# A softmax-attention and Mish kernel: order of all engines planned anew, six blocks of exps moved from ScalarE to VectorE, the second group's queries made later, the dense branch in other groups

## Chip, cores, metric

The kernel runs on one core of one Trainium2 chip. The metric is the device time of one execution in microseconds (us), lower is better. Each ratio compares runs on one chip. PE is TensorE's matmuls, PEld its weight loads, ACT is ScalarE, DVE VectorE, POOL GpSimd, SP SyncE. L891 is line 891 of the kernel; the lines of the changed kernel are numbered five higher (L896), and those of some experiments a few higher again.

## The reference

Attention with 32 heads of 20 dimensions over 2048 tokens, and beside it a dense branch with a Mish activation; a sigmoid gate per token mixes the two.

```python
def _A_ref(x, wqkv, wo):                     # x: 1 x 2048 x 640
    q, k, v = (x @ wqkv) ...                 # 32 heads of 20
    p = softmax(q k^T * 20 ** -0.5)
    return (p v) ... @ wo
def _B_ref(x, w1, b1, w2):                   # 640 -> 1536 -> 640
    h = x @ w1 + b1
    return (h * tanh(log1p(exp(h)))) @ w2    # cut: written there in its stable form
g = sigmoid((x * gate_w).sum(-1))
return g * a + (1 - g) * b                   # both on A_x
```

## The kernel before

The work is cut into 33 groups: four heads by 512 queries (the last group is halved into groups 31 and 32). A group has 16 blocks of 128 keys. For each block TensorE makes scores into a two-bank PSUM buffer (two heads of 512 queries), and either ScalarE takes exps of it, or VectorE makes an approximate exp out of integer steps; TensorE then multiplies the result with the values. `SHARE` says how many blocks of each group VectorE takes.

```python
SHARE = (3, 6, 5, 2, 5, 4, 4, 6, 3, ...)     # one number for each group
def dve_keys(G):
    n = SHARE[G]
    if G >= NG - 2:                          # the two half groups take blocks in pairs
        return [DVE_KEYS[i:i + 2] for i in range(0, n - 1, 2)]
    return [(j,) for j in (DVE_KEYS[2:2 + n] if G == 0 else DVE_KEYS[:n])]

# ScalarE: one exp for two heads of a block (1024 columns, PSUM to SBUF)
nc.scalar.activation(eb.tile[:, 0:w * QC], sb.tile[:, 0:w * QC], ACT.Exp, scale=inv)
...
te.__init__("ACT", 55 + 0.833 * w * QC, ex, [ts, prev], prio=2, key=n, rings=[eb], frees=[sb])

# VectorE: for two heads of a block, and then two shifted copies of all four
nc.vector.tensor_scalar(out=bufs[0].tile[...], in0=xb.tile, scalar1=..., scalar2=..., ...)
...
(nc.vector ...).tensor_scalar(out=bufs[i].tile[...], in0=bufs[0].tile[...], scalar1=float(SHIFTS[i]), ...)
```

All engines' instruction order is fixed while the program is built. A planner (`class Order`) holds a list of tasks with costs in ns, keeps a clock for each engine and picks the next task by priority and thresholds; the tasks are issued in the order it finds. `DENSE`, `KEYS`, `OUT` and the like say from which group on a task may be picked (`at(3.5)`: when half the exps of group 3 are issued). Where TensorE would be idle, the planner puts filler matmuls with a zero weight to keep its clock up. Three two-bank buffers (`S`) hold scores for both engines.

```python
LOW, AHEAD, HOLD, BESIDE, AHEAD_D = 2, 24, 650, 30, 2000      # one a line in the kernel
...
end = S[1].before.end or self.now["ACT"] + 908 * (S[1].key - self.exp - 1)
...
for G in list(range(1, NQ)) + [g_of(NP - 1, c) for c in range(NQ)]:
    q_unit(G, at(G - 0.85 if G > 1 else 0.15), prio=2.5, key=G)
```

The softmax here doesn't subtract the row's maximum and nothing guards it: scores larger than these inputs give would overflow.

## Time and profile before

| | before |
|---|---|
| time, median of 4 runs | 799.9 us (798.3 to 804.8) |
| span of the profiled run | 797.9 us |
| busy PE / DVE / ACT | 763.0 / 686.7 / 760.6 us |
| first exp starts; last exp ends | 11.3; 779.7 us |

The prediction below shows the busy shares, the costly groups and the waits. One more view is wanted, the busy time by stretches of the span (columns: stretch and its length, then busy us and instructions of PE, PEld, DVE, ACT and POOL, the clock, the DMA share, GB/s):

```profile
0.00:20.00 20.00, 15.98 (x198) 8.35 (x198) 6.99 (x21) 11.29 (x13) 9.24 (x10) 1.00 0.93 313
20.00:40.00 20.00, 19.15 (x418) 9.70 (x416) 16.86 (x28) 14.47 (x16) 0.00 (x0) 1.00 0.60 199
40.00:60.00 20.00, 19.63 (x290) 6.91 (x286) 17.00 (x29) 19.22 (x22) 0.00 (x0) 1.00 0.09 23
```

ScalarE is the fourth pair: 14.47 of 20 us from 20 to 40, while TensorE has 19.15. In the opening ScalarE waits for TensorE.

### The profile page before, as it was taken

Reading aid. Unit: us, or ns where it says so; the run is one execution under the profiler, and the core shown is the slowest. Engines: PE = TensorE matmul, PEld = TensorE weight load, DVE = VectorE, ACT = ScalarE, POOL = GpSimd, SP = SyncE. Lnnn points to the kernel's source line nnn. Section 1 sums busy time; section 2 is a strip of 40 time slices with the busy share of each in tenths; the row PEclk is TensorE's granted clock in tenths of the full one; section 3 lists DMA queues with packets and bytes.
Section 4 is the critical chain, followed back from the end, with each engine's and each line's share of the span. In section 5 each row is a group of like instructions: output and inputs, shape, how many; then the busy total and the mean of one; then the engine's idle time right before and its main releaser. Section 6 shows DMA issues by size and latency. Waiting matters only on the chain.

```text
span 797.9 us, 25753 instructions
## 1 busy us (share of the span) xinstructions
PE 763.0 (96%) x11326; PEld 272.7 (34%) x11326; DVE 686.7 (86%) x910; ACT 760.6 (95%) x789; POOL 9.8 (1%) x12
## 2 busy tenths in 40 slices
PE   7999999999899999899999999989999998999987
PEld 4432223323433223432333323243322233333355
DVE  3889988897799978898999998988898888989964
ACT  5799999999999999999999999999999999999991
POOL 4000000000000000000000000000000000000000
PEclk9999999999999999999999999999999999999999
DMA  9600220111011100011210121100010002202123
GB/s 312 201 23 21 46 58 21 27 36 52 28 40 38 36 19 22 6 47 38 62 42 21 31 64 44 31 23 28 23 36 17 20 19 85 69 19 82 37 67 108
DMA packets 47096, 39.88 MB, mean 50 GB/s; under 512 B 20580, under 2 KB 41252, under 8 KB 46984
## 3 DMA queue, kind: packets, MB, share of 16 engines
q1 hardware_dynamic: 46040, 37.80, 16.6%
q8 instruction: 88, 1.44, 0.7%
q10 hardware_dynamic: 944, 0.45, 0.2%
q14 instruction: 24, 0.20, 0.1%
HBM read 26.63 MB, written 11.08 MB: 47 GB/s over the span
## 4 chain that ended last, share of the span: by engine, by line
PE 49%; ACT 38%; DVE 7%; DMA 3%; issue 3%; SPq 1%; POOL 0%; DVEq 0%; ACTq 0%
ACT es L891 28%; PE S L866 18%; PE C L849 13%; PE X L585 10%; ACT arena L1072 8%; DVE t L925 3%; PE X L668 2%; PE S L585 2%; DVE t L939 1%; DMA rows<-rec 1%; DMA rbc<-rows 1%; PE X L625 1%; PE X L647 1%; ACT L1072 1%; ACT L1071 1%
## 5 line engine op out<-in xcount | busy, mean ns | idle before, releaser
L891 ACT ACTIVATE es<-S 128x1024 bf16<-128x1024 f32 x738 | 680.3, 1128 | 13.8 <-PE S L866 13.4
L925 DVE TENSOR_SCALAR t<-S 128x1024 uint16<-128x1024 f32 x286 | 348.1, 1219 | 38.9 <-PE S L866 37.4
L866 PE MATMUL S<-qs,kt 32*128 32x512 bf16 (+1 forms) x2112 | 302.6, 376 | 15.2 <-ACT es L891 11.3
L939 DVE TENSOR_SCALAR t<-t 128x2048 uint16<-128x2048 uint16 x286 | 189.3, 684 | 7.2 <-PE C L849 5.5
L866 PEld LDWEIGHTS <-kt 32*128 32x128 bf16 x2112 | 90.6, 91 | 288.3 <-issue 280.3
L849 PE MATMUL C<-es,va 128*32 128x512 bf16 (+1 forms) x1524 | 134.8, 380 | 1.0 <-DVE oraw L973 0.6
L849 PE MATMUL C<-t,vs 128*32 128x512 bf16 (+1 forms) x1176 | 102.0, 379 | 2.2 <-DVE t L939 1.6
L585 PE MATMUL X<-w,arena 128*32 128x320 bf16 x1536 | 78.3, 302 | 0.2
L585 PE MATMUL X<-xt,w 128*32 128x512 bf16 x960 | 74.8, 383 | 2.6 <-DVE arena L1058 1.4
L849 PEld LDWEIGHTS <-va 128*32 128x32 bf16 x2112 | 47.2, 95 | 66.7 <-issue 61.7
L1072 ACT ACTIVATE arena<-arena 128x2048 bf16<-128x2048 bf16 x36 | 69.2, 1944 | 0.3
L849 PE MATMUL C<-t,va 128*32 128x512 bf16 (+1 forms) x588 | 56.9, 379 | 0.0
L585 PEld LDWEIGHTS <-arena 128*32 128x32 bf16 x1856 | 40.2, 95 | 40.2 <-issue 31.6
L668 PE MATMUL X<-xt,wqk 128*32 128x512 bf16 (+1 forms) x640 | 49.5, 383 | 1.5 <-DVE g L674 1.2
L1058 DVE TENSOR_SCALAR arena<-X,b 128x512 bf16<-128x512 f32 x48 | 35.8, 745 | 6.2 <-PE X L585 6.2
L849 PEld LDWEIGHTS <-vs 128*32 128x32 bf16 x1176 | 28.5, 95 | 31.4 <-issue 27.9
L585 PEld LDWEIGHTS <-w 128*32 128x32 bf16 (+1 forms) x1280 | 27.2, 95 | 33.4 <-issue 27.8
L585 PE MATMUL X<-wvt,xt 128*32 128x160 bf16 x1240 | 27.8, 233 | 4.7 <-DVE va L725 3.9
L1026 DVE TENSOR_TENSOR on<-oraw,rbc 128x512 bf16<-128x512 f32 (+1 forms) x32 | 21.7, 679 | 11.8 <-DMA rbc<-rows 11.6
L585 PEld LDWEIGHTS <-xt 128*32 128x32 bf16 x1280 | 23.3, 96 | 15.3 <-issue 13.5
L463 PE MATMUL C<-wqk,gw 128*32 128x512 bf16 (+4 forms) x380 | 26.3, 368 | 0.0
L674 DVE CAST g<-X 120x512 bf16<-120x512 f32 x32 | 21.8, 681 | 2.1 <-PE X L668 2.1
(80 smaller groups left out, 250.6 us busy)
## 6 DMA issues: line engine op xcount, KB each, us to landing
rbc<-rows SPq DMA_DIRECT2D x124, 64.0 KB
w<-in_B_w_dram SPq DMA_DIRECT2D x2, 1920.0 KB
out_dram<-xt SPq DMA_DIRECT2D x16, 160.0 KB
oc<-on SPq DMA_DIRECT2D x112, 20.0 KB
arena<-in_A_x_dram SPq DMA_DIRECT2D x3, 640.0 KB
k<-g SPq DMA_DIRECT2D x16, 120.0 KB
kt<-k SPq DMA_DIRECT2D x24, 80.0 KB
q<-g SPq DMA_DIRECT2D x16, 120.0 KB
```

What stands on the lines that cost most here:

```text
L463: nc.tensor.matmul(t[32 * r:32 * r + 32, a:a + n], lhsT=gw[:, 0, 1:33], rhs=wqk[:, r, 0:n], start=G is None, stop=G is None, tile_position ...
L585: nc.tensor.matmul(t[32 * r:32 * r + 32, 0:width], lhsT=lhsT(r), rhs=rhs, start=a, stop=b, tile_position=(0, 32 * r))
L668: nc.tensor.matmul(t[32 * r:32 * r + w, 0:QC], lhsT=wqk[:, k, a:a + w], rhs=xt[:, c, k, :], start=k == 0, stop=k == KT - 1, tile_position= ...
L674: nc.vector.tensor_copy(out=gb.tile, in_=t[0:120, 0:QC])
L849: nc.tensor.matmul(acc[G][32 * r:32 * r + 32, qa:qb], lhsT=vs4[:, b, term - 1, DVE_KEYS.index(j), h:h + 32] if term else va4[:, b, j, h:h ...
L866: nc.tensor.matmul(t[:, (off + a) * QC + i * w:(off + a) * QC + (i + 1) * w], lhsT=kt[32 * r:32 * r + 32, (p % 2) * S + j * P:(p % 2) * S ...
L891: nc.scalar.activation(eb.tile[:, 0:w * QC], sb.tile[:, 0:w * QC], ACT.Exp, scale=inv)
L925: nc.vector.tensor_scalar(out=bufs[0].tile[:, 2 * QC * hp:2 * QC * (hp + 1)], in0=xb.tile, scalar1=P * LOG2E * inv, scalar2=P * (127 - log ...
L939: (nc.vector if eng == "DVE" else nc.gpsimd).tensor_scalar(out=bufs[i].tile[:, a * w:(a + 1) * w], in0=bufs[0].tile[:, a * w:(a + 1) * w], ...
L1026: nc.vector.tensor_tensor(out=nb.tile[:, qa:qb], in0=ob.tile[:, qa:qb], in1=rb.tile[:, qa:qb], op=ALU.mult)
L1058: lambda t: nc.vector.tensor_scalar(out=hs[:, ft, :], in0=t[:, 0:QC], scalar1=b1[:, ft:ft + 1], scalar2=None, op0=ALU.add),
L1072: nc.scalar.activation(v, hs[:, 4 * a:4 * a + 4, :] if i == 0 else v, func, bias=1.0 if i == 1 else 0.0)
```

## The change

It intends a shorter program by the same forms of instructions in another order: the planner is told a longer time for an exp (below, the new pitch), six blocks move from ScalarE to VectorE, and group 1's queries are made later. The core of the diff (left out: two `908` to `915` more, the clause for `IDLE`, which is never true, and literals that became entries of `STEPS` with the same value):

```diff
-SHARE = (3, 6, 5, 2, 5, 4, 4, 6, 3, 5, 5, 5, 5, 5, 4, 4, 6, 4, 3, 6, 5, 4, 5, 4, 5, 4, 6, 4, 5, 4, 3, 4, 4)
+SHARE = (3, 4, 5, 4, 5, 5, 5, 4, 5, 5, 5, 6, 3, 4, 4, 5, 5, 6, 4, 6, 5, 4, 4, 6, 5, 6, 6, 5, 4, 4, 3, 3, 6)
-DENSE = (1.25, 4.7, 11.7, 18.4)
+DENSE = (1.75, 4.25, 9.3, 14.95)
-MISH = (2.4, 4.2, 0.25, 3.7)
+MISH = (2.2, 4.1, 0.5, 2.55)
-DOWN = (-0.85, -1.2, 4.15, 7.5)
+DOWN = (-0.85, -0.55, 3.3, 7.0)
-KEYS = ((0, 0.8, 1.45), (1, 5.2, 7.45), (2, 13.05, 14.0), (3, 17.65, 18.85), (4, 24.55, 25.05))
+KEYS = ((0, 0.35, 1.75), (1, 5.2, 7.75), (2, 12.45, 12.8), (3, 17.8, 18.1), (4, 23.35, 23.55))
-VALUES = ((1, 3.1), (2, 10.6), (3, 12.7))
+VALUES = ((1, 4.6), (2, 10.6), (3, 12.1))
-OUT = (26.05, 27.7, 27.55)
+OUT = (29.85, 30.05, 26.65)
-    LOW = 2
+    LOW = 3
-    AHEAD = 24
+    AHEAD = 6
-    HOLD = 650
+    HOLD = 350
-    BESIDE = 30
-    AHEAD_D = 2000
+    BESIDE = 120
+    IDLE = 1000000000.0
+    AHEAD_D = 1600
-            end = S[1].before.end or self.now["ACT"] + 908 * (S[1].key - self.exp - 1)
+            end = S[1].before.end or self.now["ACT"] + 915 * (S[1].key - self.exp - 1)
-        q_unit(G, at(G - 0.85 if G > 1 else 0.15), prio=2.5, key=G)
+        q_unit(G, at(G - STEPS[4] if G > 1 else 0.45), prio=2.5, key=G)
-        te.__init__("ACT", 55 + 0.833 * w * QC, ex, [ts, prev], prio=2, key=n, rings=[eb], frees=[sb])
+        te.__init__("ACT", 62 + 0.833 * w * QC, ex, [ts, prev], prio=2, key=n, rings=[eb], frees=[sb])
```

More of the change, by code (lines that the diff above doesn't have):

```diff
@@ L34 @@
 DVE_KEYS = (1, 4, 7, 10, 13, 14)
-SHARE = (3, 6, 5, 2, 5, 4, 4, 6, 3, 5, 5, 5, 5, 5, 4, 4, 6, 4, 3, 6, 5, 4, 5, 4, 5, 4, 6, 4, 5, 4, 3, 4, 4)
-DENSE = (1.25, 4.7, 11.7, 18.4)
-MISH = (2.4, 4.2, 0.25, 3.7)
-DOWN = (-0.85, -1.2, 4.15, 7.5)
-KEYS = ((0, 0.8, 1.45), (1, 5.2, 7.45), (2, 13.05, 14.0), (3, 17.65, 18.85), (4, 24.55, 25.05))
+SHARE = (3, 4, 5, 4, 5, 5, 5, 4, 5, 5, 5, 6, 3, 4, 4, 5, 5, 6, 4, 6, 5, 4, 4, 6, 5, 6, 6, 5, 4, 4, 3, 3, 6)
[3 more added lines that the diff above has]
+KEYS = ((0, 0.35, 1.75), (1, 5.2, 7.75), (2, 12.45, 12.8), (3, 17.8, 18.1), (4, 23.35, 23.55))
 QUERIES = 2.05
-VALUES = ((1, 3.1), (2, 10.6), (3, 12.7))
-OUT = (26.05, 27.7, 27.55)
+VALUES = ((1, 4.6), (2, 10.6), (3, 12.1))
+OUT = (29.85, 30.05, 26.65)
+STEPS = (2.8, 2.0, 0.2, 0.6, 0.85, 1.7)
 PAIRS = 8
@@ L195, in pick_pe @@
         if S and S[1].before2:
-            end = S[1].before2.end or self.now["ACT"] + 908 * (S[1].key - self.exp - 2)
+            end = S[1].before2.end or self.now["ACT"] + 915 * (S[1].key - self.exp - 2)
             if not (S[1].before2.end and S[1].before2.end <= now) and len(self.spare.free) < S[1].key - self.exp:
@@ L206, in pick_pe @@
                     end = free[1][0]
-                last = 0 if self.mode == "row" else (S[1].before.end or self.now["ACT"] + 908 * (S[1].key - self.exp - 1)) - self.EARLY
+                last = 0 if self.mode == "row" else (S[1].before.end or self.now["ACT"] + 915 * (S[1].key - self.exp - 1)) - self.EARLY
                 S = max(S[0], min(end + self.LAT["ACT"], last)), S[1]
@@ L223, in pick_pe @@
         if S and S[1].before:
-            end = S[1].before.end or self.now["ACT"] + 908 * (S[1].key - self.exp - 1)
+            end = S[1].before.end or self.now["ACT"] + 915 * (S[1].key - self.exp - 1)
             over = max(lim, end - self.EARLY)
-        if X and X[1].due + self.LATE < self.visit:
+        if X and (X[1].due + self.LATE < self.visit or
+                  X[1].due <= self.visit and self.now["DVE"] + self.IDLE < now):
             lim = min(lim, X[0])
@@ L709, in q_fetch @@
         t_q[G] = o.add("SP", 4000, fetch, t_zero + [t_qd[u, c] for u in {u for _, u, _ in pieces(p)}],
-                       after=at(G - 1.7), prio=1, key=G - 0.5, rings=[q_buf[G]])
+                       after=at(G - STEPS[5]), prio=1, key=G - 0.5, rings=[q_buf[G]])
         t_q[G].issue = 1150
@@ L825 @@
         for i, js in enumerate(((0, 1, 2), (3, 4, 5), (6, 7, 8), (9, 10, 11), (12, 13, 14), (15,))):
-            v_unit(b, js, at(a + 0.2 * i), a + 0.2 * i)
+            v_unit(b, js, at(a + STEPS[2] * i), a + STEPS[2] * i)
     t_sel = o.add("POOL", 2000, make_sel, [t_k[7, j] for j in range(NS)] + list(t_kd.values()), prio=2)
@@ L1192 @@
         for ft in range(FT):
-            h_unit(c, ft, at(base + 2.8 * ft / FT), base)
+            h_unit(c, ft, at(base + STEPS[0] * ft / FT), base)
         mish(c, base + MISH[c])
@@ L1196 @@
             for hf in range(2):
-                b_unit(c, u, hf, at(base + DOWN[c] + 2.0 * (2 * u + hf) / 8), base + 4)
+                b_unit(c, u, hf, at(base + DOWN[c] + STEPS[1] * (2 * u + hf) / 8), base + 4)
     free_of = {c: [] for c in range(NQ)}
@@ L1211 @@
             for hf in range(2):
-                f_unit(c, u, hf, at(OUT[c] + 0.6 * (2 * u + hf) / 8), 29 + c)
+                f_unit(c, u, hf, at(OUT[c] + STEPS[3] * (2 * u + hf) / 8), 29 + c)
     ORDER.append(o.run())
```

## The prediction

> **What bounds the kernel now.** I read the page's busy shares first, then the slices, then the groups by line, then the waits of each engine, and last the timeline of the opening and of the end.
>
> ```profile
> PE 763.0 (96%) x11326; PEld 272.7 (34%) x11326; DVE 686.7 (86%) x910; ACT 760.6 (95%) x789; POOL 9.8 (1%) x12
> ...
> PE   7999999999899999899999999989999998999987
> PEld 4432223323433223432333323243322233333355
> DVE  3889988897799978898999998988898888989964
> ACT  5799999999999999999999999999999999999991
> ```
>
> ScalarE (ACT) has a 5 in the first slice, a 7 in the second, a 1 in the last, and nines between. Its idle time is 797.9 - 760.6 = 37.3 us. By stretches of the trace it lies so: 8.7 us in the first 20 us, 5.5 us from 20 to 40, 16.2 us after 780, 0.8 us from 760 to 780, and about 6 us in all the 720 us between. So in the body ScalarE is 99% busy: **the body lasts as long as ScalarE's work in it**.
>
> TensorE's 96% says less. 26.3 us of it (L463, 380 matmuls) are fillers that multiply a zero weight to keep the clock up, and a busy time that joins the modelled ends of short matmuls counts their latency too. VectorE has 14% free.
>
> ```profile
> L891 ACT ACTIVATE es<-S 128x1024 bf16<-128x1024 f32 x738 | 680.3, 1128 | 13.8 <-PE S L866 13.4
> L925 DVE TENSOR_SCALAR t<-S 128x1024 uint16<-128x1024 f32 x286 | 348.1, 1219 | 38.9 <-PE S L866 37.4
> ...
> L939 DVE TENSOR_SCALAR t<-t 128x2048 uint16<-128x2048 uint16 x286 | 189.3, 684 | 7.2 <-PE C L849 5.5
> ...
> L849 PE MATMUL C<-t,vs 128*32 128x512 bf16 (+1 forms) x1176 | 102.0, 379 | 2.2 <-DVE t L939 1.6
> ...
> L1072 ACT ACTIVATE arena<-arena 128x2048 bf16<-128x2048 bf16 x36 | 69.2, 1944 | 0.3
> ```
>
> The reader is to see two things. An exp lasts 1128 ns but is worth 680.3/738 = 0.922 us of the engine, since neighbours overlap. And ScalarE waited 13.4 us in all for scores (L866), while VectorE waited 37.4 us for them: the plan already serves ScalarE first.
>
> ```profile
> PEld L866 <- issue: 280.3, 732, 1.8
> ...
> ACT es L891 <- PE S L866: 13.4, 15, 2.9
> ...
> PE S L866 <- ACT es L891: 11.3, 23, 1.5
> ```
>
> Of these waits, the largest (2.9 us) is in the opening, and with the next four it makes 8.1 us between 12 and 60 us. Before it the timeline has:
>
> ```profile
> 17.57 0.61 PE L647 MATMUL X<-xt,wvt 128*32 128x512 bf16 x8
> ...
> 18.50 0.61 PE L647 MATMUL X<-xt,wvt 128*32 128x512 bf16 x8
> ...
> 24.65 1.26 PE L625 MATMUL X<-xt,wvt 128*32 128x512 bf16 x20
> ...
> 27.20 2.15 ACT L891 ACTIVATE es<-S 128x1024 bf16<-128x1024 f32 x2 [2.94 <-PE S L866]
> ```
>
> L647 here makes the second group's queries, and they sit in front of the third chunk's keys (L625 at 24.65) for which ScalarE then waits.
>
> **What the Trainium skill says.** "ScalarE: Activation LUTs", section "What ACT_TABLE_LOAD costs", gives 186 ns + 0.833 ns per element for an activation with immediate scale and bias, and says neighbours overlap by some 93 ns. For 1024 elements that is an estimated pitch of 186 + 853 - 93 = 946 ns; the trace has 922, so the slope agrees and the fixed part is a little smaller with this source. The same section gives 1283 ns for a table load; the trace's eight loads at L1071 and L1072 take 1283 each. "VectorE: DVE Perf Modes", section "The perf-mode tier table", gives 693 ns for a 2048-element bf16 tensor_scalar in SBUF and a lower mode for PSUM sources; the trace's 684 (L939) and 1219 for only half the elements out of PSUM (L925) agree. "Perfetto Trace Analysis", section "Identifying the Most-Contended Engine", says that occupancy is a fair measure for ScalarE and VectorE and that matmul busy share is not one for TensorE; the 26.3 us of fillers in this trace show why.
>
> **The change part by part.** No instruction's form changes. What changes is who takes which block of scores, and the order.
>
> (1) *The shares.* SHARE says how many of a group's 16 key blocks VectorE exponentiates. In the first 31 groups the sum goes from 139 to 145. The last two groups take blocks in pairs and round down: before 2 and 2 pairs, after 1 and 3, the same four. So six blocks move. A block is two exps on ScalarE (two of four heads each): 31 x 16 = 496 blocks, (496 - 139) x 2 + 24 = 738 exps before, which is the count in the row, and (496 - 145) x 2 + 24 = 726 after. **ScalarE loses 12 exps: 12 x 0.922 = 11.1 us.** Since it is 99% busy in the body, that is on the path.
>
> VectorE gains two L925 and two L939 a block: 6 x 2 x (1.217 + 0.662) = 22.5 us, with the busy time of each group divided by its count. It goes from 686.7 to about 709 us. Between 20 and 780 us it has 760 us and is busy about 671 now; 693 then, 91%. That lies beside ScalarE's work as long as it keeps up. TensorE's score tiles are as many as before (12 fewer for ScalarE, 12 more for VectorE); each moved block adds eight scaled-value matmuls (1176 = 8 x 147 blocks now), 48 x 102.0/1176 = 4.2 us of TensorE. It can displace fillers, of which there are 26.3 us.
>
> (2) *Order constants.* 908 to 915 ns, and 55 to 62, put the planned exp nearer to the traced 922. They change no work, only what order is found: 738 x 7 ns = 5.2 us by which the old plan let ScalarE run early. The old order already leaves only 6 us of ScalarE idle in the body, so a truer order has at most those 6 us to win there. The other thresholds (HOLD, BESIDE, AHEAD, LOW) have no sign that the profile shows; the new IDLE is so large that its clause can never be true.
>
> (3) *The opening.* The second group's queries are opened at 0.45 of the first group, not 0.15. The three pieces of L647 in front of the stall last 0.40 + 0.61 + 0.61 = 1.6 us, so the wait of 2.94 us can fall by about that. The rest of those 8.1 us has other causes, and the same matmuls have to run before group 1 needs them. I count **-2 us, between -4 and 0**.
>
> (4) *The dense branch.* Its four chunks open at 1.75, 4.25, 9.3 and 14.95, not 1.25, 4.7, 11.7 and 18.4: the same 36 activations of 1.94 us and eight table loads, in other groups. The sum on ScalarE does not change, and I expect the number of loads to stay eight, since only the first piece of Ln and of Tanh switches. What it can change is TensorE's fit: now fillers take 6.4 us in the stretch 640 to 680 and 5.1 us in 520 to 560, where the activations are thick, so the work is uneven.
>
> (5) *The end.* OUT goes from 26.05 and 27.7 to 29.85 and 30.05 for the first two chunks of the output. That looks like a delay, but now the first of their mixes (L1145 on X) runs only at 741.7 us, in the last groups anyway. From the last exp (about 779.7) to the end are 18 us of projection matmuls, mixes and stores, which the change does not touch: 0, within 1 us.
>
> The sum: -11.1 - 2, and **+2 to +3 for new waits of ScalarE**, because VectorE at 91% holds its score buffers at more awkward moments (three two-bank buffers serve both engines). Net about -10.6 us of the profiled span. On the timed median that is 801.2 - 10.6 = 790.6. Because a better-fitted order may also take a part of the 6 us of body idle, I put it at **790.0 us**, a gain of 1.4%.
>
> **The rivals.**
> *A: the work that leaves ScalarE returns as waits.* VectorE or the three shared score buffers become the bound in dense groups; ScalarE's waits for L866 rise from 13.4 to over 20 us. For it: VectorE already waited 37.4 us for scores, so TensorE cannot always serve both. Against it: the fillers show spare TensorE time. It would make 795 to 801 us.
> *B: everything falls into place.* The opening yields its 4 us and the body its idle, on top of the exps: 801.2 - 11.1 - 4 - 2 = about 784. For it: the opening's stall has one plain cause. Against it: body idle is already under 1%, and more VectorE work makes it harder to keep.
> *C: TensorE is the true bound, and ScalarE merely keeps pace.* Then 12 fewer exps are worth nothing and 4.2 us more matmuls cost: 801 to 806. For it: TensorE's slices are all nines, and from 700 to 740 both are 100% busy. Against it: 26.3 us of fillers, and ScalarE seldom waits for it.
>
> **Range and chances.** B's end lies near 783, A's near 799; I take 782 to 798 for 8 in 10. Over 2% faster means under 785.2, which takes 16 us: the exps, the whole opening and some body idle. I give that 0.19, within 2% 0.78, slower by over 2% (above 817) 0.03.
>
> **What would show each step right or wrong.** L891 x726 with busy near 669 us, and a total of ScalarE near 749.5, show (1); L925 and L939 x298 and VectorE near 709 show its other side. ScalarE's waits for L866 under 16 us keep rival A out; over 20 us are rival A. The first 40 us should hold 12 us of ScalarE idle, not 14.2, for (3). Table loads at L1071 and L1072 should be eight; each more costs 1.28 us. From the last exp to the end should be 17 to 19 us for (5). The prediction is wrong if the span stays within 3 us of the old one though the exps are 12 fewer, or if it falls by over 16 us, which no term of my sum holds.

## The result, and the profile after

The changed kernel runs at **788.4 us** (median of 4, 787.7 to 790.6) against 799.9 before (798.3 to 804.8). The ratio is 0.985, 95% interval 0.980 to 0.990. A ratio here is the mean time of one kernel's runs over that of the other's of the same rounds, so not quite the ratio of the medians. The output is right.

Of the page after, the busy shares and the groups that answer to those shown before:

```profile
PE 754.6 (96%) x11346; PEld 267.3 (34%) x11346; DVE 706.0 (90%) x934; ACT 751.3 (96%) x777; POOL 9.7 (1%) x12
...
L896 ACT ACTIVATE es<-S 128x1024 bf16<-128x1024 f32 x726 | 671.0, 1069 | 12.8 <-PE S L871 12.1
L930 DVE TENSOR_SCALAR t<-S 128x1024 uint16<-128x1024 f32 x298 | 363.2, 1220 | 21.3 <-PE S L871 19.7
...
L944 DVE TENSOR_SCALAR t<-t 128x2048 uint16<-128x2048 uint16 x298 | 197.6, 684 | 6.4 <-PE C L854 4.2
...
L854 PE MATMUL C<-t,vs 128*32 128x512 bf16 (+1 forms) x1224 | 110.4, 378 | 3.2 <-DVE t L944 3.0
...
L1077 ACT ACTIVATE arena<-arena 128x2048 bf16<-128x2048 bf16 x36 | 68.7, 1928 | 0.3
```

Twelve exps fewer (726), twelve instructions more in each of VectorE's two rows, 48 matmuls more. VectorE waits 19.7 us for scores, not 37.4. ScalarE waits 12.1 us, hardly less than 13.4.

The busy time by stretches after, the same three:

```profile
0.00:20.00 20.00, 15.82 (x254) 8.46 (x254) 8.30 (x25) 11.35 (x13) 9.24 (x10) 1.00 0.91 308
20.00:40.00 20.00, 18.75 (x354) 8.69 (x352) 14.48 (x22) 17.59 (x20) 0.00 (x0) 1.00 0.63 205
40.00:60.00 20.00, 19.99 (x298) 6.39 (x295) 19.40 (x33) 19.92 (x22) 0.00 (x0) 1.00 0.08 22
```

ScalarE has 17.59 us in the second stretch, 3.1 more. The timeline after shows the stall there shrunk:

```profile
23.32 1.26 PE L630 MATMUL X<-xt,wvt 128*32 128x512 bf16 x20
...
25.88 4.69 ACT L896 ACTIVATE es<-S 128x1024 bf16<-128x1024 f32 x5 [1.63 <-PE S L871]
```

The keys of the first heads are made in four chunks of 512. The third chunk's (then L625 at 24.65) start at 23.32 and ScalarE waits 1.63 us, not 2.94. Group 1's queries (L652) now run at 32.3 us, no longer from 15.4 to 18.9; whether that is why, experiment 4 asks.

**A ledger.** Busy and idle time cannot say where 11.3 us of span went, because a wait shorter than the tail of the exp before it is not idle: exps overlap. So I took the start of each exp from the trace, and its distance to the next start. Where nothing holds ScalarE back, that distance is the same all through: 904 ns, in 485 of the distances before and 437 after to within 5 ns (170 in each lie between 911 and 929, most of them at about 920; what sets these is not known). What is above 904 ns I call the **excess**; it is the waits, those hidden under a tail too, and those 16 ns. (Of the 13 distances that hold Mish activations or the gate's exp, what exceeds their usual length counts; that is about 2 us in each kernel, and the rows do not hang on it.)

| us | before | after | difference |
|---|---|---|---|
| start of the first exp | 11.3 | 10.6 | -0.6 |
| exps x 0.904 | 667.2 | 656.3 | **-10.9** |
| excess, 0 to 20 us | 0.1 | 0.8 | +0.7 |
| excess, 20 to 60 us | 7.5 | 3.4 | **-4.1** |
| excess, 60 to 760 us | 15.3 | 20.4 | **+5.1** |
| excess after 760 us | 1.3 | 0.1 | -1.2 |
| end of the last exp to the end | 18.3 | 18.0 | -0.3 |
| Mish activations, table loads, the rest | 76.9 | 77.0 | +0.1 |
| span | 797.9 | 786.6 | -11.3 |

In this account the 12 exps are the gain; the opening gives four more, and the body takes them back as waits. Whether the exps are also the cause, the experiments ask. (The profiled run of the kernel before had 3.41 us at half clock from 282.8 us on, beside which lie some 1.3 us of its excess; that of the changed kernel had none before its end. So without it the body's rise would be nearer to 6 us.)

### The profile page after: what moved, and what is told of

Same layout as the page of the kernel before. It is cut to its first block, busy times and chain, and to the rows that moved or that the text cites.

```text
span 786.6 us, 25802 instructions
## 1 busy us (share of the span) xinstructions
PE 754.6 (96%) x11346; PEld 267.3 (34%) x11346; DVE 706.0 (90%) x934; ACT 751.3 (96%) x777; POOL 9.7 (1%) x12
## 4 chain that ended last, share of the span: by engine, by line
PE 49%; ACT 31%; DVE 12%; DMA 3%; issue 3%; SPq 1%; POOL 0%; DVEq 0%; ACTq 0%
ACT es L896 22%; PE S L871 18%; PE C L854 14%; PE X L590 11%; ACT arena L1077 8%; DVE t L930 5%; DVE t L944 3%; PE X L673 2%; DMA rbc<-rows 2%; PE S L590 1%; DMA rows<-rec 1%; DMA wvt<-in_A_wqkv_dram 1%; ACT L1077 1%; ACT L1076 1%; DVE on L1031 1%
## 5 line engine op out<-in xcount | busy, mean ns | idle before, releaser
L896 ACT ACTIVATE es<-S 128x1024 bf16<-128x1024 f32 x726 | 671.0, 1069 | 12.8 <-PE S L871 12.1
L930 DVE TENSOR_SCALAR t<-S 128x1024 uint16<-128x1024 f32 x298 | 363.2, 1220 | 21.3 <-PE S L871 19.7
L944 DVE TENSOR_SCALAR t<-t 128x2048 uint16<-128x2048 uint16 x298 | 197.6, 684 | 6.4 <-PE C L854 4.2
L871 PEld LDWEIGHTS <-kt 32*128 32x128 bf16 x2112 | 83.6, 91 | 277.0 <-issue 266.7
L854 PE MATMUL C<-es,va 128*32 128x512 bf16 (+1 forms) x1500 | 131.0, 378 | 1.5 <-DVE oraw L978 0.8
L854 PE MATMUL C<-t,vs 128*32 128x512 bf16 (+1 forms) x1224 | 110.4, 378 | 3.2 <-DVE t L944 3.0
L854 PEld LDWEIGHTS <-va 128*32 128x32 bf16 x2112 | 49.4, 95 | 69.5 <-issue 60.7
L854 PE MATMUL C<-t,va 128*32 128x512 bf16 (+1 forms) x612 | 59.5, 377 | 0.4 <-DVE t L930 0.4
L854 PEld LDWEIGHTS <-vs 128*32 128x32 bf16 x1224 | 31.7, 95 | 36.2 <-issue 31.0
L590 PEld LDWEIGHTS <-xt 128*32 128x32 bf16 x1280 | 23.3, 96 | 15.4 <-issue 13.8
L468 PE MATMUL C<-wqk,gw 128*32 128x512 bf16 (+4 forms) x352 | 25.4, 352 | 0.0
L978 DVE COPY oraw<-C 128x512 f32<-128x512 f32 (+1 forms) x33 | 22.0, 667 | 0.7 <-PE C L854 0.6
```

The source lines that it names most:

```text
L468: nc.tensor.matmul(t[32 * r:32 * r + 32, a:a + n], lhsT=gw[:, 0, 1:33], rhs=wqk[:, r, 0:n], start=G is None, stop=G is None, tile_position ...
L590: nc.tensor.matmul(t[32 * r:32 * r + 32, 0:width], lhsT=lhsT(r), rhs=rhs, start=a, stop=b, tile_position=(0, 32 * r))
L854: nc.tensor.matmul(acc[G][32 * r:32 * r + 32, qa:qb], lhsT=vs4[:, b, term - 1, DVE_KEYS.index(j), h:h + 32] if term else va4[:, b, j, h:h ...
L871: nc.tensor.matmul(t[:, (off + a) * QC + i * w:(off + a) * QC + (i + 1) * w], lhsT=kt[32 * r:32 * r + 32, (p % 2) * S + j * P:(p % 2) * S ...
L930: nc.vector.tensor_scalar(out=bufs[0].tile[:, 2 * QC * hp:2 * QC * (hp + 1)], in0=xb.tile, scalar1=P * LOG2E * inv, scalar2=P * (127 - log ...
L944: (nc.vector if eng == "DVE" else nc.gpsimd).tensor_scalar(out=bufs[i].tile[:, a * w:(a + 1) * w], in0=bufs[0].tile[:, a * w:(a + 1) * w], ...
```

## The experiments

Theory: ScalarE bounds the body, so 12 exps fewer are 11 us. Rivals: TensorE is the true bound; the gain is the new order's and not the exps'; the new planned pitch alone is enough. Twelve kernels ran, on four chips, each with its own runs of the kernel before (medians 800.1, 799.5, 798.4 and 798.7). The last table of this section has them all.

### 1. As much less for ScalarE in both kernels, order untouched

Each exp runs on 1006 of 1024 columns. The planner's cost is not changed, so all engines' orders stay. (The columns that are left out are set once at the start.)

```diff
-            nc.scalar.activation(eb.tile[:, 0:w * QC], sb.tile[:, 0:w * QC], ACT.Exp, scale=inv)
+            nc.scalar.activation(eb.tile[:, 0:w * QC - 18], sb.tile[:, 0:w * QC - 18], ACT.Exp, scale=inv)
```

> The kernel before with its order untouched, each of its 738 exps shortened by 18 of 1024 columns (15 ns at 0.833 ns a column, so 738 x 15 = 11.1 us less for ScalarE, the same as the 12 exps that the change takes away). Results are wrong on purpose. Theory (ScalarE is the bound of the body): the time falls by 9 to 11 us, ratio to the kernel before 0.986 to 0.989, though nothing was planned anew. Rival C (TensorE is the true bound): it stays within 3 us, ratio above 0.996. Rival 'the new order, not the smaller share, brings the gain': ratio above 0.993.

> The changed kernel, order untouched, its 726 exps shortened by the same 18 columns: 726 x 15 = 10.9 us less for ScalarE. If ScalarE is still the bound after the change, the time falls by 8 to 11 us, to 777 to 780 us, ratio to the kernel before 0.971 to 0.976, and ScalarE's waits for scores grow by under 3 us. If VectorE or TensorE has become a bound beside it, under half of it comes (above 783 us), and ScalarE's waits grow by over 5 us.

Measured: the kernel before goes to 794.8 us, ratio 0.994 (0.991 to 0.998); the changed one to 785.3, ratio 0.9815 (0.979 to 0.984). The rows of exps, first of the one before, then of the changed one:

```profile
L894 ACT ACTIVATE es<-S 128x1006 bf16<-128x1006 f32 x738 | 672.8, 1068 | 16.7 <-PE S L869 15.5
```

```profile
L899 ACT ACTIVATE es<-S 128x1006 bf16<-128x1006 f32 x726 | 665.6, 1029 | 13.9 <-PE S L874 12.8
```

The distance of exps that nothing holds back is now 888 ns, so the cut itself arrived: 16 ns each, 11.8 and 11.6 us. But the excess rose, from 24.2 to 31.4 us and from 24.7 to 32.2. The idle column shows only a part of that (15.5 us against 13.4, and 12.8 against 12.1). **This speaks against my theory as I had put it**: the same cut gives 5.4 of 11.8 us in the old order, 3 to 4 of 11.6 in the new (3.1 by the medians, 4.0 by the spans). By the marks set beforehand, 0.994 is the reading "the new order, not the smaller share" (over 0.993), though with an interval that reaches into the gap between it and the theory; and 785.3 is the reading that another engine bounds beside ScalarE, though the waits of over 5 us that were to show it appear in the excess (7.5 us) and not in the idle column (0.7). ScalarE is a bound of the body, but not the only one.

### 2. Which engine takes it back

Here the changed kernel is made lighter on the other engines, order untouched. For TensorE the value matmuls (all but a group's first and last) run on 480 of 512 columns; for VectorE its two steps run on 500 of 512 columns a head in 30 of the 33 groups, and the value matmuls are 12 columns shorter with them.

```diff
+                cut = 32 if 0 < k < total - 1 and G < NG - 2 else 0
-                    nc.tensor.matmul(acc[G][32 * r:32 * r + 32, qa:qb],
+                    nc.tensor.matmul(acc[G][32 * r:32 * r + 32, qa:qb - cut],
```

```diff
+                m = QC if G in (13, NG - 2, NG - 1) else QC - 12
                 nc.vector.tensor_scalar(
-                    out=bufs[0].tile[:, 2 * QC * hp:2 * QC * (hp + 1)], in0=xb.tile,
+                    out=bufs[0].tile[...].rearrange("p (h q) -> p h q", q=QC)[:, :, 0:m],
+                    in0=xb.tile.rearrange("p (h q) -> p h q", q=QC)[:, :, 0:m],
```

> The changed kernel, order untouched; 724 of the weighted-value steps (all but a group's first and last) run on 480 of 512 columns, so TensorE has 724 x 32/2.4 ns = 9.7 us less to do and ScalarE and VectorE the same. Wrong results on purpose. If TensorE bounds the body beside ScalarE, the time falls by 2 to 6 us below 788.4 (ratio 0.977 to 0.983) and ScalarE's excess over back-to-back exps, 24.7 us in the changed kernel, falls. If ScalarE alone is the bound, it stays within 1.5 us and the excess stays at 23 to 26 us.

> The lighter TensorE and the exps of 1006 columns together, order untouched; wrong on purpose. The shorter exps alone gave 3 us of 10.9 in the changed kernel. If it was TensorE's load that took the rest back, the same cut is now worth 6 us or more over the run with the lighter TensorE alone, and the time is under 779 us (ratio under 0.973). If it was the fixed order itself (a score that comes late because of what stands before it, not because TensorE is full) or VectorE, the cut is worth 2 to 4 us again, and the time is 780 to 784.

> The changed kernel, order untouched, with the exps of 1006 columns (10.9 us less for ScalarE) and VectorE's two steps on 500 of 512 columns a head in 30 of the 33 groups (25 + 13 ns for 282 pairs of instructions, 10.6 us less; the matmuls that read them are 12 columns shorter, 3.8 us less for TensorE). Wrong on purpose. The shorter exps alone gave 785.3 us, with a lighter TensorE 782.8. If VectorE took the rest back, the time is 776 to 780 us (ratio 0.970 to 0.976). If it did not, it is 782 to 785 (above 0.977).

> All three at once, order untouched: ScalarE 10.9 us less, VectorE 10.6 us less, TensorE about 10 us less. Wrong on purpose. If the three engines bound different stretches of one tight order, only this gives the whole cut: 776 to 779 us, ratio 0.970 to 0.974. If something that none of the three cuts touches takes it back (the times from one engine to the next, transfers, the dense branch's matmuls), it stays at 780 to 783.

Measured: 786.1, 782.8, 781.2 and 778.8 us (ratios 0.982, 0.978, 0.978, 0.976; the first two and the last two on one chip each). The cuts arrived: a step of four value matmuls starts 202 to 203 ns after the one before it where it was 216 (32 columns at 0.42 ns), and VectorE's two steps take 1195 and 672 ns on average, not 1220 and 684. The row of exps with all three lighter:

```profile
L900 ACT ACTIVATE es<-S 128x1006 bf16<-128x1006 f32 x726 | 660.5, 1048 | 12.5 <-PE S L875 12.1
```

A lighter TensorE alone gives 2 us, by the ratios (0.985 to 0.982), of the 9.7 taken off, and the excess falls to 22.9 us: just inside the reading "TensorE bounds beside ScalarE". With the shorter exps as well, the excess is 31.6 us, and with shorter exps and a lighter VectorE 30.3: hardly under the 32.2 of the shorter exps alone. (Both traces have a stretch of 3.4 us at half clock in the opening, with 1.5 us more of excess in the first 20 us than the changed kernel; the second has one more at 110 us.) So neither TensorE nor VectorE alone holds back the cut, and the two expectations are no clean "yes": 782.8 was within "the fixed order or VectorE", 781.2 between the two ranges. With all three lighter the excess is 25.6 us, about that of the changed kernel, and the span is 10.1 us shorter for cuts of 10 to 11.6. By the ratios (0.985 to 0.976) it is only about 7 us, with 4 us of uncertainty on the first ratio alone; 778.8 lies in the range set for "only all three give the whole cut", 0.976 above it (0.970 to 0.974). So most of the cut comes, and whether all of it does is not shown; a part may be taken back by what no cut touched, such as the times from one engine to the next. On one chip, the shorter exps give 3.3 us beside the lighter TensorE (786.1 to 782.8), and the lighter TensorE gives 2.3 us beside the other two (781.2 to 778.8): each of these adds about a quarter of itself. **The three engines share the bound**: that each is the last at some places of this order is the reading that fits, and ScalarE's time alone counts at about a third.

### 3. The fillers

The fillers on the accumulator are left out; order untouched.

```diff
-            for r in range(4):
+            for r in range(4 if G is None else 0):
                 nc.tensor.matmul(t[32 * r:32 * r + 32, a:a + n], lhsT=gw[:, 0, 1:33], rhs=wqk[:, r, 0:n],
```

> The changed kernel, order untouched, without the filler matmuls on the accumulator (about 25 us of TensorE's busy time). If they only lie in TensorE's spare time (so the change's 48 added matmuls have room) the time stays within 2 us of the changed kernel's 788, ratio 0.983 to 0.988, and TensorE's busy time falls by over 15 us. If TensorE is the bound, the time falls by over 5 us. If the clock is granted less without them, the clock in the records falls below 0.98 and the time rises.

Measured: 798.4 us, ratio 0.998 (0.994 to 1.001): 10 us slower than the changed kernel. The clock by slices and the mean clock, the page's line and the list of cores:

```profile
PEclk9999989999999999989999999989999999899999
```

```profile
core 0: 798.4 us, clock 0.983
```

The trace has four stretches of 6.83 us at half clock in the body, where the changed kernel's profiled run has none before its end. Excess: 35.9 us. As the order is the same, each exp can be set against the same exp of the changed kernel: from the first exp to the last it falls back by 11.2 us, of which 8.6 at these four stretches. So the third reading is right in kind, though the clock (0.983 in the profiled run, 0.983 to 0.991 in all four) stayed just above the 0.98 that was set: left out and replaced by nothing, the fillers cost clock. Whether real work may take their place is another question, which this does not test; the changed kernel has 48 value matmuls more and 28 fillers fewer (352, not 380) at a clock of 0.999.

### 4. The opening

The changed kernel with one number set back; all is planned anew.

```diff
-        q_unit(G, at(G - STEPS[4] if G > 1 else 0.45), prio=2.5, key=G)
+        q_unit(G, at(G - STEPS[4] if G > 1 else 0.15), prio=2.5, key=G)
```

> The changed kernel with the second group's queries opened at 0.15 again, not 0.45; the whole order is planned anew from that, so later parts differ too. Step 3 of the prediction: ScalarE's idle time in the first 40 us rises by 1 to 4 us (it is 11.1 us in the changed kernel, 14.2 in the one before), and the time with it, to 789 to 793 us. Rival (the opening's gain comes from the other order constants): the first 40 us stay at 11 to 12 us of idle. The time beyond the first 60 us may move by a few us either way, as a plan that was tuned as a whole is disturbed.

Measured: 794.1 us, ratio 0.992 (0.989 to 0.995), a little above the range set. ScalarE's idle time in the first 40 us is 13.9 us, 2.8 more than in the changed kernel, as expected. Its stretch from 20 to 40 us:

```profile
20.00:40.00 20.00, 19.21 (x398) 9.14 (x390) 16.55 (x26) 15.26 (x18) 0.00 (x0) 1.00 0.60 196
```

ScalarE is busy 15.26 us there, 17.59 in the changed kernel; the excess in the stretch is 5.2 against 2.8 us. Later kernels agree: with the late queries 2.8 us (experiment 5's old shares, and the searched one), with the early ones 6.1 and 6.2 (the other two of experiment 5), 6.2 in the kernel before; but those differ in other numbers too. So the later queries are worth **2.4 us** there, the plan around them included.

Not by the wait that the prediction named, though. With the queries early again (L652), the exp after the third chunk's keys still waits only 1.65 us, and the loss lies at the fourth chunk's:

```profile
19.04 1.05 PE L652 MATMUL X<-xt,wvt 128*32 128x512 bf16 x16
...
23.85 1.25 PE L630 MATMUL X<-xt,wvt 128*32 128x512 bf16 x20
...
26.40 5.61 ACT L896 ACTIVATE es<-S 128x1024 bf16<-128x1024 f32 x6 [1.65 <-PE S L871]
...
32.14 1.43 PE L630 MATMUL S<-xt,wvt 128*32 128x512 bf16 x20
...
35.09 5.69 ACT L896 ACTIVATE es<-S 128x1024 bf16<-128x1024 f32 x6 [3.09 <-PE S L871]
```

In the changed kernel the fourth chunk's keys start at 29.17, in two pieces, and the exp after them waits less:

```profile
29.17 0.61 PE L630 MATMUL S<-xt,wvt 128*32 128x512 bf16 x8
...
30.09 0.83 PE L630 MATMUL S<-xt,wvt 128*32 128x512 bf16 x12
...
32.27 8.36 ACT L896 ACTIVATE es<-S 128x1024 bf16<-128x1024 f32 x9 [0.79 <-PE S L871]
```

So the fall from 2.94 to 1.65 us at the third chunk comes without the late queries, from other numbers of the change, and the late queries save 2.3 us at the fourth (3.09 to 0.79; 2.10 in the kernel before). The profiled span is 4.3 us longer than the changed kernel's: 2.3 us of excess from 20 to 60 us, 0.5 us of a later first exp, and some 1.5 us beyond 60 us, where the plan is disturbed. (By the ratios the kernel is some 5.7 us slower; the profiled run was the fastest of its four.)

### 5. The shares, the pitch, and fewer exps in an order not tuned to them

Each is planned anew from other numbers: the changed kernel with `SHARE` of before; the kernel before with the new pitch alone; the kernel before with the new `SHARE`, `DENSE`, `MISH`, `DOWN`, `KEYS`, `VALUES` and `OUT` but the old pitch, thresholds and opening.

```diff
-SHARE = (3, 4, 5, 4, 5, 5, 5, 4, 5, ...)    # the changed kernel
+SHARE = (3, 6, 5, 2, 5, 4, 4, 6, 3, ...)    # with the shares of before
```

```diff
-        te.__init__("ACT", 55 + 0.833 * w * QC, ...    # the kernel before; 908 likewise
+        te.__init__("ACT", 62 + 0.833 * w * QC, ...    # with the new pitch alone; 915 likewise
```

> The changed kernel with SHARE as before: 738 exps, planned anew with the new constants and places. Theory (the 12 exps are the gain): 10.9 us more of ScalarE, 797 to 803 us, ratio 0.995 to 1.003. Rival (order and places bring the gain): 787 to 792, ratio under 0.990. Since a plan tuned as a whole is disturbed, ScalarE's excess may rise too; it is counted apart from the exps.

> The kernel before with the new pitch alone (915 for 908 ns, 62 for 55) and planned anew. If the truer pitch by itself brings the gain: 786 to 792 us, ratio under 0.990. Theory: it takes no work from ScalarE, the count stays 738, and the time is 796 to 806, ratio 0.995 to 1.007.

> The kernel before with the new SHARE and the new places of the dense branch, keys, values and output, but the old pitch, order constants and opening; planned anew. It has 726 exps. If fewer exps are enough, whatever the order, it runs at 787 to 792 us like the changed kernel (ratio under 0.990). If the gain needs an order that keeps ScalarE fed, ScalarE's excess over back-to-back exps rises well above 25 us and the time is 794 to 806 us.

None isolates its number cleanly, as a plan that was tuned as a whole is disturbed each time. Measured: old shares 811.8 us (ratio 1.015, 1.010 to 1.020); the pitch alone 807.4 (1.011, 1.005 to 1.017); new shares and places 800.6 (1.003, 1.001 to 1.004, 20 runs). The first two are slower than any range set for them (797 to 803, and 796 to 806). The row of exps of the last:

```profile
L891 ACT ACTIVATE es<-S 128x1024 bf16<-128x1024 f32 x726 | 672.3, 1094 | 24.5 <-PE S L866 22.4
```

It has the 726 exps and gains nothing: its excess is 37.7 us, 13.5 more than before, which eats the 10.9 us. With the pitch alone the excess is 31.5 us with 738 exps. With the old shares it is 34.8, so of the 22.8 us of span by which that kernel is behind the changed one, 10.9 are the exps and 10.1 the excess (this profile had 10.2 us at half clock, so up to 5 us of that may be the clock's), and 2 lie after the last exp. **Neither fewer exps nor the pitch alone is the gain; it is fewer exps in an order that keeps the excess where it was.** Not tested is the rival that remains: an order tuned as long for the old shares.

### 6. A further search

Nothing above beats the changed kernel and is right. So I searched further over the same numbers, by the planner's own clock, and ran the best: one block given back (728 exps), the fourth dense chunk at 17.55, `LOW` 4, `HOLD` 500, `BESIDE` 170 and others.

```diff
-DENSE = (1.75, 4.25, 9.3, 14.95)
+DENSE = (1.65, 4.2, 9.05, 17.55)
-    HOLD = 350
+    HOLD = 500
```

> The changed kernel's planner with further searched numbers (one block given back to ScalarE, so 728 exps; the fourth dense chunk at 17.55; other starts and thresholds), found with the planner's own clock, which puts its end 2 us earlier than the changed kernel's. If that clock holds for ScalarE's excess, the time is 785 to 788 us, ratio 0.982 to 0.985, against 0.985 of the changed kernel. If the clock is no guide at this size, it lands anywhere between 786 and 797 us with an excess over back-to-back exps of 25 to 35 us.

Measured: 792.2 us (6 runs), ratio 0.990 (0.987 to 0.992): faster than before, slower than the changed kernel. Where the planner and the trace have the last exp end:

```
                        planner   trace
before                   770.2    779.7
changed                  768.9    768.7
changed, queries 0.15    772.8    773.2
changed, old shares      780.1    789.4
before, pitch alone      781.0    786.8
before, shares, places   778.6    782.0
searched                 767.8    774.6
```

The planner is right to 0.4 us for the changed kernel and its neighbour, and 3 to 10 us short for the others, in part with the new pitch too. (The searched profile had two stretches of 3.4 us at half clock, which explain at most 3.4 of its 6.8; the 10.2 us of the old shares' profile explain up to 5 of its 9.3.) So a plan whose end is 2 us better by that clock is not known to be better; only the chip says.

### All runs

| kernel | exps | excess | span | median | ratio to before |
|---|---|---|---|---|---|
| before | 738 | 24.2 | 797.9 | 799.9 | 1 |
| changed | 726 | 24.7 | 786.6 | 788.4 | 0.985 |
| before, exps of 1006 columns | 738 | 31.4 | 792.3 | 794.8 | 0.994 |
| changed, exps of 1006 columns | 726 | 32.2 | 782.6 | 785.3 | 0.982 |
| changed, without fillers | 726 | 35.9 | 798.4 | 798.4 | 0.998 |
| changed, queries at 0.15 | 726 | 28.7 | 790.9 | 794.1 | 0.992 |
| changed, lighter TensorE | 726 | 22.9 | 784.6 | 786.1 | 0.982 |
| changed, shorter exps and lighter TensorE | 726 | 31.6 | 781.5 | 782.8 | 0.978 |
| changed, shorter exps and lighter VectorE | 726 | 30.3 | 780.2 | 781.2 | 0.978 |
| changed, all three lighter | 726 | 25.6 | 776.5 | 778.8 | 0.976 |
| changed, old shares | 738 | 34.8 | 809.4 | 811.8 | 1.015 |
| before, new pitch alone | 738 | 31.5 | 805.1 | 807.4 | 1.011 |
| before, new shares and places | 726 | 37.7 | 799.4 | 800.6 | 1.003 |
| searched further | 728 | 28.3 | 791.4 | 792.2 | 0.990 |

Excess and span are of the profiled run; the median is of all runs. The rows with shorter or lighter steps compute a wrong result on purpose.

## Why the prediction was right, and where it was not

The time, 788.4 us, lies beside the 790.0 predicted and within 2% of the kernel before, as thought likeliest. The gain is the one predicted; the reason given for it holds only in part, and two misses that cancel helped. By its steps:

- **The shares (1).** Right in count and size: 726 exps, -10.9 us for -11.1. The 0.922 us that an exp was "worth" was 2% too high: it was busy time over count, and holds hidden waits; the distance of unhindered exps is 0.904. That is also why the exps' busy time fell by 9.3 us only. VectorE came to 706.0 us (709 predicted), its two rows by 23.4 us (22.5 predicted).
- **"On the path", since ScalarE is 99% busy.** Too simple. Experiments 1 and 2 show three engines bound together; the same cut without a new order gives half, and experiment 5 shows 12 exps fewer for nothing. The 11 us came whole only because the new order also held the excess. That the step ended at the right number is in part luck: the order came with it.
- **The order constants (2).** I gave a truer order "at most those 6 us to win". That asked the wrong thing: its worth is not in idle that it removes but in waits that do not appear. Nor is the new pitch "nearer": 922 ns was busy time over count. The distances up to 930 ns have a mean of 908 ns before and 909 after, so the old 908 was right and 915 is some 7 ns too long; what it gives the plan is slack, not truth. By itself it costs 7 to 9 us (experiment 5).
- **The opening (3).** Right that the later queries help, wrong in where. The named wait fell by 1.3 us (1.6 said), but it does so with early queries too; the late ones pay at the fourth chunk's keys (experiment 4). -2 us was too small: -3.4 in the stretch from 20 to 40, of which experiment 4 puts 2.4 on the queries. Idle of ScalarE in the first 40 us is 11.1 us, where I said 12.
- **The dense branch (4) and the end (5).** As said: still eight table loads; the last exp to the end 18.3 and 18.0 us. OUT was no delay: the first mix comes at 734.3 us, before at 741.7.
- **New waits, +2 to +3.** Under-sized: the body's excess rose by 5.1 us. The row of waits hides it (12.1 us, under the 16 that I set as the mark). The opening's surplus and this miss cancel within a microsecond or so, which is luck.
- **The fillers as spare time**, used against rival C and for the 4.2 us of added matmuls: not shown. 28 fillers went, but only 0.9 us of their busy time (26.3 to 25.4), and without them the clock falls (experiment 3), so their 26.3 us are no measure of what TensorE can spare. Rival C is wrong as stated, since with 12 exps fewer and 48 matmuls more the kernel became faster, but it had a true core: TensorE is one of three.

What stays open: whether an order tuned for the old 738 exps could gain as much, and which of the single thresholds (`LOW`, `AHEAD`, `HOLD`, `BESIDE`) keeps the excess low. Each single number set back disturbs the whole plan by several microseconds, so taking them one by one would not tell.

## What to carry to other kernels

When three engines are each 90 to 96% busy in a fixed order, taking work off one was worth a quarter to a half of it here with the order untouched; test a "bound" by shortening its instructions with the order untouched before trusting its busy share. Count waits from the distances between starts, not from idle time: overlapping tails hide them. And choose between plans on the chip, as a planner's clock that fits one plan to 0.2 us can miss the next by 7.

## What the Trainium skill lacked or had wrong

- "ScalarE: Activation LUTs", section "What ACT_TABLE_LOAD costs", names no memory for its fixed cost, and the 946 ns that I had estimated from it in the prediction is too long for a source in PSUM: 904 measured. "Perfetto Trace Analysis", section "Optimizing Scalar/DVE Operations", gives some 51 ns of overhead for ScalarE on PSUM, with which the runs agree closely: 0.833 x 1024 + 51 = 904 ns, and 0.833 x 1006 + 51 = 889 against 888 measured.
- "ScalarE: Activation LUTs", section "What ACT_TABLE_LOAD costs", puts a switch at about 2.66 us, 1283 ns and a drain of 1380. In these traces the load takes 1283 ns, starts 17 ns after the activation before it ends, and the next activation starts 1294 ns after it. Two 2048-element activations start 3.22 to 3.23 us apart with a load between them and 1.80 without: a switch costs 1.42 to 1.43 us here.
- "TensorE: Matmul & The Clock Gate", section "HAM oscillation", puts the rule for keeping the clock as no idle gap of over some 3.4 us. Here so long a gap was not needed: the first of the four stretches at half clock without the fillers, at 102.3 us, came after 3.4 us in which TensorE was busy for 2.71 and never idle for more than 0.6 us. Before all 15 stretches (of 3.41 or 6.83 us, those at the very end left out) that these profiles hold, TensorE was busy for 0.63 to 2.75 us of the last 3.41, with no gap above 2.78. What is too little activity is not shown: 3.41 us with only 1.71 of work (from 184.5 us, the same run) passed at full clock. The page reports, right after that section, a kernel throttled by many short gaps.
- No page says that a busy time by union hides waits shorter than the overlap of neighbours: exps of one shape last 1002 to 1230 ns in the changed kernel at an unhindered pitch of 904, and 7.5 us more of waiting (experiment 1, changed kernel) showed as 0.7 us more idle.
